# Relaying the opening of a fused attention and feed-forward kernel

## Chip, cores and metric

The kernel runs on one NeuronCore of a Trainium2 chip. The metric is the device time of one execution in microseconds (us), taken as the median of several runs. The profile is one execution recorded by the hardware profiler; its own span is a little shorter than the measured time (431.2 us against 433.38 us).

Engines and their short names: PE (TensorE, matmuls; PEld is its weight load), DVE (VectorE), ACT (ScalarE), POOL (GpSimd), SP (SyncE, which here only issues transfers).

## What is computed

Attention with normalised queries and keys over 8 batches, 12 heads, 448 positions and 64 dimensions, and then a feed-forward layer with a leaky activation on the 3584 x 768 result:

```python
def rmsnorm(x, g):
    rms = np.sqrt(np.mean(x * x, axis=-1, keepdims=True) + 1e-06)
    return x / rms * g
q_n, k_n = (rmsnorm(q, g_q), rmsnorm(k, g_k))
scores = (1.0 / np.sqrt(64)) * np.matmul(q_n, k_n.transpose(0, 1, 3, 2))
scores = scores - np.max(scores, axis=-1, keepdims=True)
attn = np.exp(scores)
attn = attn / (np.sum(attn, axis=-1, keepdims=True) + 1e-09)
x = np.matmul(attn, v)           # then heads side by side: 3584 x 768
h = x @ w_in                     # w_in: 768 x 2048
out = np.maximum(0.01 * h, h) @ w_out   # w_out: 2048 x 768
```

## The kernel before

Work is cut into 24 **units** of four heads of one batch. A unit goes through these steps:

- load q and k (SP) and v (POOL, with a conversion to 16 bits);
- squares (`prep_sq` on ACT, `prep_sqp` on POOL), their sums (`prep_ssq`, DVE), the factor 1/rms as exp(-0.5 ln) (`prep_rinv`, two ACT instructions), the multiplication (`prep_norm`, DVE);
- transposition of the normed q and k (`prep_tr`: seven matmuls into PSUM each, then a copy to SBUF on DVE or ACT; q gets the gains on the way);
- scores in seven steps t (`qk`, PE), the exponentials of each step (`ex`, ACT). The exponential needs a shift, which is taken from the maxima of step 0: `shift_max` (DVE), a matmul that spreads it (`shift_mm`, PE), two small DVE instructions, the last of which writes `eb`;
- sums of the exponentials (`zsum`) and the product with v (`pv`), both PE; 1/sum as Ln and Exp (`zinv`, ACT); the product of both (`xmul`, DVE).

Three units make a batch, and a batch's feed-forward matmuls are then fed between the attention steps of later units. That regular loop starts with unit 3. What the change touches is the hand-laid order ahead of it, in which the scheduler is switched off: each engine runs its instructions in the order of the program text.

The helpers that the text below speaks of:

```python
raws = ctx.enter_context(tc.tile_pool(name="raws", bufs=3))   # raw q, k: 3 units
# squares: 3 buffers in turn for q and k together; normed n16: 1 buffer
n16=([P, 2, NS, 2, D], FP16, 1), ...
def aux(shape, dtype, name):                                  # PSUM: 4 banks in turn
    return psum.tile(shape, dtype, tag="aux", bufs=4, name=name)
def slot():                                                   # PSUM: 2 pairs of banks for scores
    return psum.tile([P, 2, 512], FP32, tag="sT", bufs=2, name="sT")

def prep_sq(u, c=ALL, tis=BOTH):
    for ti in tis:
        nc.scalar.activation(buf(u, f"sq{ti}")[:, :, c[0]:c[1]], raw[u][ti][:, :, c[0]:c[1]], AF.Square)

def prep_sqp(u, tis=BOTH):
    for ti in tis:
        nc.gpsimd.tensor_tensor(buf(u, f"sq{ti}"), raw[u][ti], raw[u][ti], op=ALU.mult)

def prep_norm(u, c=ALL, tis=BOTH):      # two inputs in SBUF: the raw rows and the factors
    ...
        nc.vector.tensor_tensor(buf(u, "n16")[...], src[:, :, c[0]:c[1]], buf(u, "rinv")[... broadcast], op=ALU.mult)

def prep_tr(u, ti, copies):             # all chunks through one PSUM tile
    tp = aux([P, NS, P], FP16, "tp")
    for (lo, hi), copy in copies:
        for x in range(lo, hi):
            nc.tensor.transpose(tp[:, x, :], buf(u, "n16")[:, ti, x]..., ident16)
        copy(buf(u, "qkT")[:, ti, lo:hi], tp[:, lo:hi], ti == 0)

def gate(u):    # POOL copies the last element of the normed k: what follows on POOL waits for it
    nc.gpsimd.tensor_copy(gate_t, buf(u, "n16")[:, 1, NS - 1, 1, D - 1:D])

def warm(n, bank):                      # n matmuls whose result is not used
    for x in range(n):
        nc.tensor.matmul(bank[:, P:2 * P], onesp, onesp, start=True, stop=True)

def score0(u):                          # step 0 of the scores, in two aux banks
    banks = [aux([P, 512], FP32, "s0") for a in range(2)]
    score(u, 0, banks)
    st[u]["sT"] = [(0, banks)]
```

The opening itself can be read from the minus and blank-led lines of the diff below; CA, CB, K0 and K1 are chunks of the seven tiles of a unit: 0 to 3, 4 to 6, 0 alone, and 1 to 6.

Of the kernel before, what the change touches and what calls it, by code (L numbers as in the profile page):

```python
# [18 lines left out]
def kernel(  # L19
# [35 lines left out]
    def aux(shape, dtype, name):  # L55
        return psum.tile(shape, dtype, tag="aux", bufs=4, name=name)
# [30 lines left out]
    def load_w_in(n0, n):  # L87
        for a in range(2):
            for r in range(2):
                nc.gpsimd.dma_start(win16[64 * a:64 * a + 64, :, r, n0:n0 + n], win_v[a, :, :, r, n0:n0 + n])  # L90
# [19 lines left out]
    def load_v(u):  # L110
        nc.gpsimd.dma_start(vts[u % NV].rearrange("p a t d -> p a (t d)"), rows(v, u))  # L111
# [9 lines left out]
    def buf(u, name):  # L121
        if name not in st[u]:
            shape, dtype, bufs = SHAPES[name]
            st[u][name] = prep_p.tile(shape, dtype, tag=name[:2] if bufs == 3 and name != "qkT" else name, bufs=bufs, name=name)
        return st[u][name]
# [7 lines left out]
# [3 lines that stand above are left out]
# [4 lines left out]
    def prep_ssq(u, c=ALL, tis=BOTH):  # L140
        for ti in tis:
            nc.vector.tensor_reduce(buf(u, "ssq")[:, ti, :, c[0]:c[1]], buf(u, f"sq{ti}")[:, :, c[0]:c[1]],  # L142
                                    axis=AXL.X, op=ALU.add)

    def prep_rinv(u, tis=BOTH):
        x = slice(tis[0], tis[-1] + 1)
        nc.scalar.activation(buf(u, "uu")[:, x], buf(u, "ssq")[:, x], AF.Ln, bias=eps_t, scale=1.0 / D)
        nc.scalar.activation(buf(u, "rinv")[:, x], buf(u, "uu")[:, x], AF.Exp, bias=0.0, scale=-0.5)  # L148

    def prep_norm(u, c=ALL, tis=BOTH):  # L150
        n = c[1] - c[0]
        for ti in tis:
            src = raw[u][ti]
            nc.vector.tensor_tensor(  # L154
                buf(u, "n16")[:, ti, c[0]:c[1]].rearrange("p s a d -> p a s d"), src[:, :, c[0]:c[1]],
                buf(u, "rinv")[:, ti, :, c[0]:c[1], None].broadcast_to([P, 2, n, D]), op=ALU.mult)

    def prep_tr(u, ti, copies):
# [3 lines that stand above are left out]
                nc.tensor.transpose(tp[:, x, :], buf(u, "n16")[:, ti, x].rearrange("p a d -> p (a d)"), ident16)  # L162
            copy(buf(u, "qkT")[:, ti, lo:hi], tp[:, lo:hi], ti == 0)
# [21 lines left out]
    def qk(u, steps):  # L185
        st[u]["sT"] = []
        for t in steps:
            sT = slot()
            score(u, t, (sT[:, 0], sT[:, 1]))
            st[u]["sT"].append((t, sT))  # L190

    def ex(u):
        s = st[u]
        if "et" not in s:
            s["et"] = epool.tile([P, NS, 2, S], FP16, tag="et", name="et")
        for t, sT in s["sT"]:
            if isinstance(sT, list):
                for a in range(2):
                    nc.scalar.activation(s["et"][:, t, a], sT[a][:, 0:S], AF.Exp, bias=s["eb"], scale=1.0)
            else:  # L200
                nc.scalar.activation(s["et"][:, t], sT[:, :, 0:S], AF.Exp, bias=s["eb"], scale=1.0)  # L201

    def score0(u):
# [4 lines that stand above are left out]
    def shift_max(u):  # L208
        s = st[u]
        sT = s["sT"][0][1]  # L210
        if isinstance(sT, list):
            pm2 = small.tile([P, 2], FP32, tag="pm2", name="pm2")
            for a in range(2):
                nc.vector.tensor_reduce(pm2[:, a:a + 1], sT[a][:, 0:S], axis=AXL.X, op=ALU.max)
            s["spare"] = sT[0]
            nc.vector.tensor_reduce(s["spare"][:, 511:512], pm2, axis=AXL.X, op=ALU.max)
        else:
            s["spare"] = sT[:, 0]
            nc.vector.tensor_reduce(s["spare"][:, 511:512], sT[:, :, 0:S], axis=AXL.XY, op=ALU.max)  # L219
        s["dg"] = small.tile([P, P], FP16, tag="dg", name="dg")  # L220
        nc.vector.tensor_tensor(s["dg"], ident16, s["spare"][:, 511:512].broadcast_to([P, P]), op=ALU.mult)

    def shift_bank(u):
        st[u]["pb"] = aux([P, 512], FP32, "pb")
# [17 lines left out]
    def gate(u):  # L242
        nc.gpsimd.tensor_copy(gate_t, buf(u, "n16")[:, 1, NS - 1, 1, D - 1:D])
# [11 lines left out]
    def zsum_slot(u):  # L255
        s = st[u]
        s["zslot"] = slot()
        s["zt"] = [s["zslot"][:, r] for r in range(2)]
        zsum(u)
# [48 lines left out]
    def zinv(u):  # L308
        s = st[u]
        s["rz"] = zpool.tile([P, 2, S], FP32, tag="rz", name="rz")  # L310
        if "zslot" in s:
            nc.scalar.activation(s["rz"], s["zslot"][:, :, 0:S], AF.Ln)
            nc.scalar.activation(s["rz"], s["rz"], AF.Exp, bias=0.0, scale=-1.0)
        else:
            for r in range(2):
                nc.scalar.activation(s["rz"][:, r], s["zt"][r][:, 0:S], AF.Ln)
                nc.scalar.activation(s["rz"][:, r], s["rz"][:, r], AF.Exp, bias=0.0, scale=-1.0)

    def pv(u, t0=0, t1=NS):
        s = st[u]  # L320
        if t0 == 0 and "pslot" not in s:
            s["pv"] = [aux([P, 512], FP32, "pv") for r in range(2)]
        for t in range(t0, t1):
            for r in range(2):
                for a in range(2):
                    nc.tensor.matmul(s["pv"][r][64 * a:64 * a + 64, 0:S], vts[u % NV][64 * r:64 * r + 64, a, t],  # L326
                                     s["et"][64 * r:64 * r + 64, t, a], start=(t == 0), stop=(t == NS - 1))
# [244 lines left out]
    def warm(n, bank):  # L572
        for x in range(n):
            nc.tensor.matmul(bank[:, P:2 * P], onesp, onesp, start=True, stop=True)

    with tc.manual_schedule():
# [19 lines left out]
        nc.vector.tensor_copy(gcol, gps[:, 0:1])  # L596
        prep_ssq(0, ALL, (1,))
        prep_rinv(0, (1,))
        prep_sqp(1, (0,))
        load_v(0)  # L600
        load_v(1)
        prep_norm(0, CA, (0,))
        prep_norm(0, CB, (0,))
        prep_tr(0, 0, ((CA, acopy), (CB, acopy)))
        prep_norm(0, K0, (1,))
        tpk = aux([P, NS, P], FP16, "tp")

        def trk(c, copy):
            for x in range(*c):
                nc.tensor.transpose(tpk[:, x, :], buf(0, "n16")[:, 1, x].rearrange("p a d -> p (a d)"), ident16)  # L610
            copy(buf(0, "qkT")[:, 1, c[0]:c[1]], tpk[:, c[0]:c[1]])

        trk(K0, vcopy)
        prep_norm(0, K1, (1,))
        qk(0, STEPS[0])
        shift_max(0)
        trk(K1, acopy)
        load(3)
        prep_sqp(1, (1,))
        gate(0)  # L620
        load_w_in(0, 1024)
        prep_sqp(2)
        shift_bank(0)
        warm(12, st[0]["pb"])
        shift_mm(0)
        load_v(2)
        prep_ssq(1, ALL, (0,))

        def feed(u):
            load(u + 4)  # L630
            gate(u + 1)
            prep_sqp(u + 3)
            load_v(u + 3)

        def trn(u, ti, copy):
            prep_tr(u, ti, ((ALL, copy),))
# [2 lines left out]
            zsum(u, t0, t1)  # L639
            pv(u, t0, t1)  # L640

        def close(u):
            n = u + 1
            zsum_slot(u)
            ex(n)
            qk(n, (1,))
            pv(u)
            zinv(u)

        ex(0)  # L650
        prep_ssq(1, ALL, (1,))
        prep_rinv(1)
        prep_norm(1)
        prep_ssq(2)
        feed(0)
        load_w_in(1024, 1024)
        wb = aux([P, 512], FP32, "warm")
        qk(0, (1,))
        ex(0)
        warm(16, wb)  # L660
        qk(0, (2,))
        ex(0)
        warm(12, wb)
        qk(0, (3,))
        ex(0)
        warm(6, wb)
        qk(0, (4,))
        ex(0)
        trn(1, 0, vcopy)
        trn(1, 1, acopy)  # L670
        qk(0, (5,))
        ex(0)
        qk(0, (6,))
        ex(0)
        prep_rinv(2)
        score0(1)
        shift_max(1)
        shift_bank(1)
        warm(20, st[1]["pb"])
        shift_mm(1)  # L680
        close(0)

        prep_norm(2)
        prep_ssq(3)
        ex(1)
        feed(1)
        for f in range(2):
            load_w_out(8 * f, 8)
# [8 lines left out]
        ex(1)  # L697
        qk(1, (5,))
        ex(1)
        prep_rinv(3)  # L700
        score0(2)
        shift_max(2)
        qk(1, (6,))
# [1 line left out]
        shift_bank(2)  # L705
        warm(12, st[2]["pb"])
        shift_mm(2)
        close(1)

        prep_norm(3)  # L710
        ex(2)
        feed(2)
        qk(2, (2,))
        ex(2)
# [133 lines left out]
```

The softmax here doesn't subtract the row's maximum and nothing guards it: scores larger than these inputs give would overflow.

## Time and profile before

| | |
|---|---|
| measured time | 433.38 us, median of 3 runs (433.32 to 433.84) |
| span of the profiled execution | 431.2 us |
| PE, ACT, DVE, POOL busy | 409.3, 306.5, 273.2, 86.6 us |
| exponentials of 128x896 | 166, 1005 ns each on the mean |
| GpSimd squares of 128x896 | 1.67 to 1.82 us each |
| first exponential of unit 0, 1, 2, 3 | 17.23, 28.07, 36.99, 49.20 us |

"Busy" counts the time in which an engine executes; a transfer that an engine issues is not counted. A row of the timeline merges neighbouring instructions of one kind: its second column is then their busy time together, and the number after the x says how many they are. The bracket at its end gives how long the engine stood idle before the row, and whose result ended that. The column of the granted clock is the share of its full clock that TensorE was given. The share of the DMA comes out over 1 in some windows.

### The profile page before, as it was taken

The numbers are of one execution on the slowest core, as the hardware profiler recorded it, in microseconds if no ns is written. First come the engines' busy times: TensorE is split into PE (matmuls) and PEld (weight loads), VectorE is DVE, ScalarE is ACT, GpSimd is POOL, SyncE is SP. The second block draws the span as 40 slices with busy tenths as digits, with TensorE's granted clock in tenths as the row PEclk, the third lists the DMA queues.
The fourth block names the chain that finished last, engine by engine and source line by source line (L and its number), as shares of the span: only waits on it lengthen the run. The fifth ranks groups of instructions, "written<-read, shape, count | busy, mean of one in ns | idle before, by whom it ended". The sixth has DMA issues, their size and how long they took to land.

```text
span 431.2 us, 8844 instructions
## 1 busy us (share of the span) xinstructions
PE 409.3 (95%) x3645; PEld 211.2 (49%) x3645; DVE 273.2 (63%) x434; ACT 306.5 (71%) x466; POOL 86.6 (20%) x77
## 2 busy tenths in 40 slices
PE   7677999999989999999999999999999999999996
PEld 6545444445444544454445544454445444455553
DVE  5898656888659865487369864587359840542162
ACT  5389888757986779966986789966986757643400
POOL 2885423300002102112102102111101101010000
PEclk9699999999999999999999999999999999999999
DMA  8999993789566896578555797488572460212013
GB/s 264 198 239 252 237 254 85 143 170 221 154 104 114 194 206 161 143 128 212 156 103 136 170 209 171 130 141 194 160 109 44 118 143 16 44 38 73 2 44 103
DMA packets 66476, 62.37 MB, mean 145 GB/s; under 512 B 35716, under 2 KB 61572, under 8 KB 66436
## 3 DMA queue, kind: packets, MB, share of 16 engines
q1 hardware_dynamic: 55840, 49.62, 46.7%
q0 software_dynamic: 10272, 11.80, 17.8%
q8 instruction: 28, 0.46, 0.4%
q10 hardware_dynamic: 324, 0.39, 0.3%
q14 instruction: 12, 0.10, 0.1%
HBM read 45.61 MB, written 11.01 MB: 131 GB/s over the span
## 4 chain that ended last, share of the span: by engine, by line
PE 63%; ACT 16%; DVE 12%; issue 3%; ACTq 0%; DVEq 0%
PE hps L347 25%; ACT et L201 8%; PE ma L427 7%; PE md L427 6%; PE sT L182 5%; PE sT L326 4%; PE op L387 4%; PE mc L427 4%; DVE n L154 3%; PE mb L427 3%; ACT gt L341 3%; PE zc L269 3%; DVE ssq L142 1%; DVE sT L219 1%; ACT x L281 1%
## 5 line engine op out<-in xcount | busy, mean ns | idle before, releaser
L201 ACT ACTIVATE et<-sT,eb 128x896 f16<-128x896 f32 x166 | 158.6, 1005 | 15.6 <-PE sT L182 13.3
L347 PE MATMUL hps<-xt,win 128*128 128x448 f16 x756 | 151.0, 353 | 0.2 <-DVE xt L335 0.2
L347 PEld LDWEIGHTS <-win 128*128 128x128 f16 x756 | 70.6, 98 | 71.4 <-issue 9.9
L341 ACT ACTIVATE gt<-hps 128x448 f16<-128x448 f32 x126 | 65.7, 541 | 20.1 <-PE hps L347 19.4
L306 POOL TENSOR_TENSOR xt<-x,rz 128x896 f16<-128x896 f32 x16 | 33.5, 2092 | 150.8 <-DMA rz<-zs 49.8
L154 DVE TENSOR_TENSOR n<-rq,rinv 128x896 f16<-128x896 f32 (+2 forms) x25 | 27.5, 1102 | 48.4 <-ACT rinv L148 44.9
L182 PE MATMUL sT<-qkT 64*64 64x448 f16 x664 | 52.6, 366 | 4.8 <-ACT et L201 4.3
L142 DVE TENSOR_REDUCE ssq<-sq 128x14 f32<-128x896 f32 (+2 forms) x49 | 50.1, 1055 | 1.2 <-ACT sq L131 1.2
L427 PEld LDWEIGHTS <-sa 128*128 128x128 f16 x352 | 32.8, 98 | 26.3 <-issue 6.1
L281 ACT COPY x<-sT 128x896 f32<-128x896 f32 x19 | 17.2, 907 | 39.5 <-DVE sT L232 39.5
L111 POOL DMA_DIRECT2D vt<-in_v_dram x24 | 18.2, 760 | 114.4 <-PE sT L326 106.9
L427 PEld LDWEIGHTS <-gt 128*128 128x128 f16 x264 | 25.2, 98 | 20.3 <-issue 4.4
L219 DVE TENSOR_REDUCE sT<-sT 128x1 f32<-128x896 f32 x22 | 24.0, 1093 | 17.5 <-PE sT L182 17.5
L182 PEld LDWEIGHTS <-qkT 64*64 64x64 f16 x672 | 15.8, 104 | 39.0 <-issue 35.9
L387 PE MATMUL op<-wout,gt 128*128 128x384 f16 x192 | 34.1, 327 | 0.0
L427 PE MATMUL ma<-wout,gt 128*128 128x384 f16 x176 | 32.3, 326 | 0.1
L154 DVE TENSOR_TENSOR n<-rk,rinv 128x896 f16<-128x896 f32 (+2 forms) x25 | 30.1, 1206 | 0.0
L326 PE MATMUL sT<-et,vt 64*64 64x448 f16 x532 | 28.5, 349 | 0.3
L408 DVE TENSOR_TENSOR sa<-gt 128x512 f16<-128x512 f16 (+1 forms) x15 | 8.1, 543 | 29.6 <-ACT gt L341 29.6
L326 PEld LDWEIGHTS <-vt 64*64 64x64 f16 x672 | 20.4, 107 | 10.8 <-issue 1.1
L387 PEld LDWEIGHTS <-gt 128*128 128x128 f16 x192 | 17.7, 98 | 14.0 <-issue 3.2
L453 ACT COPY ost<-ma 128x384 f32<-128x384 f32 x11 | 5.3, 480 | 23.6 <-PE ma L427 23.6
(87 smaller groups left out, 444.9 us busy)
## 6 DMA issues: line engine op xcount, KB each, us to landing
rq<-in_q_dram SPq DMA_DIRECT2D x24, 448.0 KB, 5.0
rk<-in_k_dram SPq DMA_DIRECT2D x24, 448.0 KB, 5.9
out_dram<-ost SPq DMA_DIRECT2D x52, 192.0 KB, 3.8
rz<-zs SPq DMA_DIRECT2D x38, 224.0 KB, 3.3
vt<-in_v_dram POOLq DMA_DIRECT2D x24, 224.0 KB, 5.0
win<-in_moe_w_in_dram POOLq DMA_DIRECT2D x8, 384.0 KB, 9.4
wout<-in_moe_w_out_dram POOLq DMA_DIRECT2D x2, 1536.0 KB, 23.7
out_dram<-ost SPq DMA_DIRECT2D x4, 96.0 KB, 2.1
```

What stands on the lines that cost most here:

```text
L142: nc.vector.tensor_reduce(buf(u, "ssq")[:, ti, :, c[0]:c[1]], buf(u, f"sq{ti}")[:, :, c[0]:c[1]], axis=AXL.X, op=ALU.add)
L154: nc.vector.tensor_tensor(buf(u, "n16")[:, ti, c[0]:c[1]].rearrange("p s a d -> p a s d"), src[:, :, c[0]:c[1]], buf(u, "rinv")[:, ti, :, ...
L182: nc.tensor.matmul(banks[a][64 * r:64 * r + 64, 0:S].rearrange("p (t x) -> p t x", t=NS), kT(u, r, a, t), qT(u, r, a), start=True, stop=True)
L201: nc.scalar.activation(s["et"][:, t], sT[:, :, 0:S], AF.Exp, bias=s["eb"], scale=1.0)
L219: nc.vector.tensor_reduce(s["spare"][:, 511:512], sT[:, :, 0:S], axis=AXL.XY, op=ALU.max)
L281: nc.scalar.copy(s["x32"], s["pslot"][:, :, 0:S])
L306: eng.tensor_tensor(xts[b][:, g], s["x32"], s["rz"], op=ALU.mult)
L326: nc.tensor.matmul(s["pv"][r][64 * a:64 * a + 64, 0:S], vts[u % NV][64 * r:64 * r + 64, a, t], s["et"][64 * r:64 * r + 64, t, a], start=(t ...
L341: nc.scalar.activation(dst, src, AF.Prelu, bias=0.0, scale=1.0, alpha=0.01)
L347: nc.tensor.matmul(hps[:, 0:S], win16[:, kt // 2, kt % 2, ts(ft, P)], xt[:, kt // 2, kt % 2], start=(kt == 0), stop=(kt == KT - 1))
L387: nc.tensor.matmul(op2[:, 0:HC], gt[:, ft, ds(col(t), P)], wout16[:, ft, ds(HC * half, HC)], start=(ft == 0), stop=(ft == FT - 1))
L427: nc.tensor.matmul(bank[:, 0:HC], a[:, f], b[:, f], start=(first and f == 0), stop=(f == HF - 1), skip_group_check=not first)
```

## The change

It reorders the opening, from unit 0's norms to the start of unit 2's exponentials:

- **GpSimd gated.** Its first squares, those of unit 1, are taken from it; its first instruction after the set-up is now the gate on unit 0's norms. The squares of unit 1 are computed on ACT. The loads of v and of w_in are put at other places of POOL's queue: v of unit 0 ahead of the squares of unit 2, v of units 1 and 2 after the first half of w_in, the second half of w_in ahead of the squares of unit 3.
- **Transposes through separate tiles.** The two chunks of unit 0's q get a PSUM tile each, and its k is normed in full ahead of the copy of its first tile. In unit 1 the copy of q moves from DVE to ACT and k is handled in two chunks on DVE.
- **Shifts earlier.** The step 0 scores and the shift of unit 1 are computed among the exponentials of unit 0; the sums, factors and norms of unit 2 come after the shift of unit 1 instead of before, and so with unit 3 and unit 2.
- **Fewer warm-up matmuls.** 20 fewer ahead of the shift of unit 1, 6 fewer ahead of that of unit 0, and others moved.

The diff, whole:

```diff
--- before.py
+++ after.py
@@ -596,35 +596,39 @@
         nc.vector.tensor_copy(gcol, gps[:, 0:1])
         prep_ssq(0, ALL, (1,))
         prep_rinv(0, (1,))
-        prep_sqp(1, (0,))
-        load_v(0)
-        load_v(1)
         prep_norm(0, CA, (0,))
         prep_norm(0, CB, (0,))
-        prep_tr(0, 0, ((CA, acopy), (CB, acopy)))
         prep_norm(0, K0, (1,))
-        tpk = aux([P, NS, P], FP16, "tp")
-
-        def trk(c, copy):
-            for x in range(*c):
-                nc.tensor.transpose(tpk[:, x, :], buf(0, "n16")[:, 1, x].rearrange("p a d -> p (a d)"), ident16)
-            copy(buf(0, "qkT")[:, 1, c[0]:c[1]], tpk[:, c[0]:c[1]])
-
-        trk(K0, vcopy)
         prep_norm(0, K1, (1,))
+
+        def tr(u, ti, chunks, tp=None):
+            if tp is None:
+                tp = aux([P, NS, P], FP16, "tp")
+            for c, copy in chunks:
+                for x in range(*c):
+                    nc.tensor.transpose(tp[:, x, :], buf(u, "n16")[:, ti, x].rearrange("p a d -> p (a d)"), ident16)
+                copy(buf(u, "qkT")[:, ti, c[0]:c[1]], tp[:, c[0]:c[1]], ti == 0)
+            return tp
+
+        tr(0, 0, ((CA, acopy),))
+        tr(0, 0, ((CB, acopy),))
+        tpk = tr(0, 1, ((K0, vcopy),))
+        prep_sq(1, ALL, (0,))
         qk(0, STEPS[0])
         shift_max(0)
-        trk(K1, acopy)
+        tr(0, 1, ((K1, acopy),), tpk)
+        prep_sq(1, ALL, (1,))
         load(3)
-        prep_sqp(1, (1,))
         gate(0)
+        load_v(0)
+        prep_sqp(2)
         load_w_in(0, 1024)
-        prep_sqp(2)
+        load_v(1)
+        load_v(2)
         shift_bank(0)
-        warm(12, st[0]["pb"])
+        warm(6, st[0]["pb"])
         shift_mm(0)
-        load_v(2)
-        prep_ssq(1, ALL, (0,))
+        prep_ssq(1)
 
         def feed(u):
             load(u + 4)
@@ -639,50 +643,48 @@
             zsum(u, t0, t1)
             pv(u, t0, t1)
 
-        def close(u):
-            n = u + 1
-            zsum_slot(u)
-            ex(n)
-            qk(n, (1,))
-            pv(u)
-            zinv(u)
-
         ex(0)
-        prep_ssq(1, ALL, (1,))
-        prep_rinv(1)
-        prep_norm(1)
-        prep_ssq(2)
-        feed(0)
-        load_w_in(1024, 1024)
-        wb = aux([P, 512], FP32, "warm")
+        prep_rinv(1, (0,))
         qk(0, (1,))
         ex(0)
-        warm(16, wb)
+        prep_rinv(1, (1,))
+        prep_norm(1, ALL, (0,))
+        prep_norm(1, K0, (1,))
+        prep_norm(1, K1, (1,))
+        load(4)
+        gate(1)
+        load_w_in(1024, 1024)
+        prep_sqp(3)
+        load_v(3)
+        wb = aux([P, 512], FP32, "warm")
+        warm(12, wb)
         qk(0, (2,))
         ex(0)
-        warm(12, wb)
+        warm(16, wb)
         qk(0, (3,))
+        tr(1, 0, ((ALL, acopy),))
+        tpk = tr(1, 1, ((K0, vcopy),))
         ex(0)
-        warm(6, wb)
         qk(0, (4,))
         ex(0)
-        trn(1, 0, vcopy)
-        trn(1, 1, acopy)
+        tr(1, 1, ((K1, vcopy),), tpk)
+        score0(1)
+        shift_max(1)
         qk(0, (5,))
         ex(0)
         qk(0, (6,))
         ex(0)
+        shift_bank(1)
+        shift_mm(1)
+        prep_ssq(2)
+        ex(1)
+        qk(1, (1,))
+        ex(1)
+        zsum_slot(0)
+        pv(0)
         prep_rinv(2)
-        score0(1)
-        shift_max(1)
-        shift_bank(1)
-        warm(20, st[1]["pb"])
-        shift_mm(1)
-        close(0)
-
+        zinv(0)
         prep_norm(2)
-        prep_ssq(3)
-        ex(1)
         feed(1)
         for f in range(2):
             load_w_out(8 * f, 8)
@@ -697,7 +699,6 @@
         ex(1)
         qk(1, (5,))
         ex(1)
-        prep_rinv(3)
         score0(2)
         shift_max(2)
         qk(1, (6,))
@@ -705,10 +706,16 @@
         shift_bank(2)
         warm(12, st[2]["pb"])
         shift_mm(2)
-        close(1)
+        prep_ssq(3)
+        ex(2)
+        qk(2, (1,))
+        ex(2)
+        zsum_slot(1)
+        pv(1)
+        prep_rinv(3)
+        zinv(1)
 
         prep_norm(3)
-        ex(2)
         feed(2)
         qk(2, (2,))
         ex(2)
```

## Prediction

> **What bounds the kernel now.** I read the busy shares first, then the windows table, to see where the bounding engine is not full, and then the merged timeline of that part.
>
> The first page section says that TensorE is busy for 95% of the span:
>
> ```profile
> span 431.2 us, 8844 instructions
> PE 409.3 (95%) x3645; PEld 211.2 (49%) x3645; DVE 273.2 (63%) x434; ACT 306.5 (71%) x466; POOL 86.6 (20%) x77
> ```
>
> The table of windows (columns: window, length, busy time of PE, PEld, DVE, ACT, POOL with counts, granted clock, DMA share, GB/s) separates two regimes:
>
> ```profile
> 10.00:20.00 10.00, 6.15 (x54) 4.59 (x55) 7.94 (x10) 3.04 (x6) 9.07 (x11) 0.66 0.95 202
> 20.00:30.00 10.00, 7.88 (x126) 5.22 (x128) 9.12 (x14) 8.36 (x12) 7.84 (x10) 1.00 1.12 240
> 30.00:40.00 10.00, 7.88 (x136) 4.72 (x125) 8.31 (x15) 9.79 (x15) 6.81 (x8) 1.00 1.11 248
> ...
> 229.00:289.00 60.00, 59.52 (x533) 29.50 (x532) 41.52 (x68) 47.56 (x70) 9.87 (x8) 1.00 0.71 151
> ```
>
> From about 49 us PE is busy 59.5 of 60 us: PE alone bounds it. Before that PE waits, and part of its work is warm-up matmuls. There the exponentials on ACT should be the bound, but ACT is busy for only 3.0 us between 10 and 20 us. The change touches only this opening. If the opening ends X us sooner, and nothing later runs short, the kernel ends X us sooner. So I follow four milestones, the first exponentials of units 0 to 3, in the timeline (columns: start, duration, engine, line, operation, out<-in, count, idle before it and its releaser):
>
> ```profile
> 8.50 1.82 POOL L135 TENSOR_TENSOR sq<-rq 128x896 f32<-128x896 f32 x1 [7.18 <-DMA rq<-in_q_dram]
> 8.69 1.77 DVE L154 TENSOR_TENSOR n<-rk,rinv 128x128 f16<-128x128 f32 x1
> 10.92 3.48 DVE L154 TENSOR_TENSOR n<-rk,rinv 128x768 f16<-128x768 f32 x1
> 11.89 1.69 POOL L135 TENSOR_TENSOR sq<-rk 128x896 f32<-128x896 f32 x1
> 14.33 1.09 DVE L219 TENSOR_REDUCE sT<-sT 128x1 f32<-128x896 f32 x1
> ...
> 17.23 1.01 ACT L201 ACTIVATE et<-sT,eb 128x896 f16<-128x896 f32 x1 [1.12 <-DVE eb L240]
> ...
> 28.07 1.16 ACT L199 ACTIVATE et<-s,eb 128x448 f16<-128x448 f32 x2 [1.61 <-DVE eb L240]
> ...
> 36.99 1.16 ACT L199 ACTIVATE et<-s,eb 128x448 f16<-128x448 f32 x2
> ...
> 49.20 1.01 ACT L201 ACTIVATE et<-sT,eb 128x896 f16<-128x896 f32 x1 [1.09 <-DVE eb L240]
> ```
>
> The DVE norm of 128 columns took 1.77 us and that of 768 columns 3.48 us, while the 896-column norms elsewhere take 1.08 to 1.09 us. Both long ones end right after a GpSimd square does (10.32 and 13.58 us). The score maximum stands behind them until 14.33 us.
>
> [...] 3.48 us is the wait until 13.58 plus 0.8 us of own work. [...] the trace has 951 ns for the square of 896. [...] the trace shows 0.66 in the window where PE stood still from 11.4 to 14.5 us.
>
> **The change, milestone by milestone.** Durations are those of the same rows in the trace before: exponential 0.92 us each in a row (4.58/5), Ln and Exp of the sums 1.82 us, ln/exp pair of one norm factor 0.45 to 0.55 us, sum of squares 1.03 us, norm 1.09 us, square on GpSimd 1.69 us.
>
> *Unit 0, first exponential.* Without GpSimd's squares the 128- and 768-column norms take about 0.25 and 0.93 us (0.8 of work plus start). DVE: norms done at 8.7 + 0.25 + 0.93 = 9.85 us, copy of K0 until 10.05. ACT's second copy of q no longer waits for the first to free the transposing tile and ends near 9.98. Scores at 10.1 instead of 11.06, maximum at 10.55 instead of 14.33, and 2.25 us from its start to the exponential (1.09, then diagonal, matmul, reduction, bias; 1.12 as in later units): **12.8** instead of 17.23. ACT meanwhile does the new squares, 0.95 each, and the K1 copy, 0.8: 9.98 + 0.9 + 1.05 + 0.95 = 12.75 us; just hidden. Gain 4.4.
>
> *Unit 0 to 1.* ACT: 7 x 0.92 + two pairs of norm factors (1.0) + the copy of q (0.92) + about 0.8 of waiting = 9.1 us. The wait: GpSimd's second square of unit 2 needs the buffer that the first sum of unit 1 frees (13.85), so it runs 13.9 to 15.6; the norm of q of unit 1, ready at 14.85, waits for it and ends at 16.7; its transposes and copy end at 18.25, while the third exponential ended at 16.65. The shift of unit 1: copies done at 19.1, then 2.57 us (as 25.50 to 28.07 before) = 21.65, under the last exponential, which ends at 21.9. First exponential of unit 1 at **21.9** instead of 28.07. Period 9.1 against 10.84, gain 1.7. The missing 20 warm-up matmuls cost nothing, if the clock stays up.
>
> *Unit 1 to 2.* Here the change gives something back. The sums and factors of unit 2 now come after the shift of unit 1, so its norms start at 21.9 + 2.1 (three exponentials) + 0.6 (factors) = 24.65, that is 2.7 us into the unit; before, 0.15 us ahead of it. DVE then: two norms to 26.75, two copies to 28.0, xmul to 29.15, and 2.50 us from the score maxima to the exponential (34.49 to 36.99 before): **31.65**. ACT would be done at 31.0. Period 9.75 against 8.92: loss 0.8.
>
> *Unit 2 to 3.* The factors of unit 3 move into this unit (0.55 on ACT), and its norms, at 34.35 to 36.45, now end after Ln and Exp (36.1), so the scores behind their transposes hold one exponential up by 0.55: period 12.2 + 1.1 = 13.3. First exponential of unit 3 at **45.0** instead of 49.20.
>
> Sum without a further collision: 4.4 + 1.7 - 0.8 - 1.1 = 4.2 us.
>
> *A likely collision.* The second half of w_in now stands on GpSimd ahead of the squares of unit 3, and its last two issues wait until the first two quarters of the first half have landed. Issued at 15.6 us, with 6.7 to 8 us to landing as before, that is 23 to 25 us; the squares then run in 23.5 to 28, across the norms of unit 2 (24.65 to 26.75), on the DVE chain that sets the next milestone. If DVE is first, nothing; if GpSimd gets in between, 1.7 us; if both squares go first, up to 3. I take 1.2. Expected gain **3.0**: 433.4 - 3.0 is about 430.3 us.
>
> The PE instructions after the opening are the same in the same order, so I carry the gain through unchanged.
>
> **Rivals.** (1) *DMA is the bound of the opening*: its share is over 1.0 from 20 us on, so the data could come no sooner. Against it: in the waits up to 62 us DMA holds up only the first squares (7.2 us on GpSimd, which is not on the path, and 1.2 and 0.5 us on ACT). But the DMA engines idle near 15 us in the new order, as w_in is issued 1 us later. If w_in or w_out were late, the gain would be gone: about 433. w_out landed at 54 and 63.5 us and the second half is first needed near 78, so there are 14 us of room. (2) *GpSimd collides repeatedly* in units 1 and 2 and the clock falls for want of warm-up: gain 0 to 1. (3) *No collision*, and waits that I counted are hidden: 427.5 to 429. (4) *PE rate after the opening absorbs it*: only if units 3 and 4 wait for sums or loads; they now have fewer us of lead on DVE.
>
> **Range and chances.** 4.2 without the collision and 1.2 with it at its worst bracket the centre; with 0.8 us for my reading of the chains on each side, 428.2 to 432.6 us. 2% would be 8.7 us, more than the whole of what the opening waits for (ACT's waits between 8 and 50 us add up to 11 us, of which 4.8 and 1.6 are attacked), so faster by over 2% gets 0.03. Slower by 2% would take two new long waits: 0.01. Within 2%: 0.96.
>
> **What would show it.** The norms of unit 0 at 0.25 and 0.93 us; first exponentials near 12.8, 21.9, 31.7 to 33, and 45 to 46.5 us; a norm of unit 1 of about 1.8 us beside a GpSimd square; the norms of unit 2 at 24.6 us, long if GpSimd's squares of unit 3 fall there; PE busy 59.5 of 60 us afterwards and the same distance from unit 3's first exponential to the end (382 us). Wrong it would be if that distance grows, which would mean late weights or late norms, or if the clock is at half in units 0 and 1.

## The result and the profile after

The changed kernel takes 431.9 us (median of 4 runs, 431.43 to 432.87) against 433.35 us before; the ratio is 0.9972, with a 95% interval of 0.9956 to 0.9989. It is faster by 1.45 us on the medians (0.5 to 1.9 us by the interval), about half of what was predicted, though the time itself lies inside the predicted range.

The head of the profile page of the changed kernel shows a shorter span and PE as busy as before:

```profile
span 430.1 us, 8784 instructions
PE 410.4 (95%) x3613; PEld 209.2 (49%) x3613; DVE 271.8 (63%) x436; ACT 308.7 (72%) x470; POOL 83.1 (19%) x75
```

The merged timeline of its opening (start, duration, engine, line, operation, out<-in, count, idle before it and releaser) has the rows that answer to those shown of before (rows between them are left out):

```profile
8.84 1.15 DVE L154 TENSOR_TENSOR n<-rk,rinv 128x128 f16<-128x128 f32 x2
10.62 1.10 DVE L219 TENSOR_REDUCE sT<-sT 128x1 f32<-128x896 f32 x1 [0.49 <-PE sT L182]
12.99 1.01 ACT L201 ACTIVATE et<-sT,eb 128x896 f16<-128x896 f32 x1 [0.30 <-DVE eb L240]
14.03 1.68 POOL L135 TENSOR_TENSOR sq<-rk 128x896 f32<-128x896 f32 x1 [1.26 <-DVE ssq L142]
14.86 1.79 DVE L154 TENSOR_TENSOR n<-rq,rinv 128x896 f16<-128x896 f32 x1
...
22.56 1.19 ACT L199 ACTIVATE et<-s,eb 128x448 f16<-128x448 f32 x2
...
23.67 0.63 POOL L90 DMA_DIRECT2D win<-in_moe_w_in_dram  x1 [2.05 <-DMA win<-in_moe_w_in_dram]
24.31 1.69 POOL L135 TENSOR_TENSOR sq<-rq 128x896 f32<-128x896 f32 x1
25.20 3.40 DVE L154 TENSOR_TENSOR n<-rq,rinv 128x896 f16<-128x896 f32 x1 [1.15 <-issue]
25.95 1.69 POOL L135 TENSOR_TENSOR sq<-rk 128x896 f32<-128x896 f32 x1
28.52 1.08 DVE L154 TENSOR_TENSOR n<-rk,rinv 128x896 f16<-128x896 f32 x1
...
34.36 1.16 ACT L199 ACTIVATE et<-s,eb 128x448 f16<-128x448 f32 x2 [0.97 <-DVE eb L240]
...
48.14 1.01 ACT L201 ACTIVATE et<-sT,eb 128x896 f16<-128x896 f32 x1 [1.09 <-DVE eb L240]
```

The two norms of unit 0's k now take 1.15 us together, where they had taken 1.77 and 3.48. The first exponentials of units 0 and 1 come 4.2 and 5.5 us sooner than before. Then the gain melts: 2.6 us at unit 2, 1.1 us at unit 3. The row that stands out is the norm of q of unit 2, at 25.20 us: 3.40 us for what takes 1.09 us elsewhere. It ends at 28.60, that is 0.96 us after GpSimd's second square (25.95 + 1.69 = 27.64). From unit 3's first exponential to the end it is 430.1 - 48.14 = 382.0 us, as before (431.2 - 49.20 = 382.0); in the profiles of all runs below it is 381.9 to 382.4 us. Whatever the opening gains or loses is passed on whole.

A second thing stands out. The windows of one us of the changed kernel (the third column from the end is the granted clock, the second number after the window PE's busy time) show half the clock twice, at 11.3 to 18.1 us and at 21.5 to 28.3 us:

```profile
12.00:13.00 1.00, 0.84 (x7) 0.26 (x7) 0.61 (x4) 0.70 (x2) 0.77 (x1) 0.50 0.91 266
...
19.00:20.00 1.00, 0.38 (x4) 0.12 (x5) 0.98 (x2) 1.00 (x3) 1.00 (x3) 1.00 1.01 158
...
24.00:25.00 1.00, 1.00 (x19) 0.57 (x14) 0.04 (x1) 0.97 (x3) 0.98 (x2) 0.50 1.12 244
```

The kernel before was at half clock once in its opening, from 13.2 to 20.0 us, so only the second stretch is new:

```profile
15.00:16.00 1.00, 1.00 (x12) 1.00 (x11) 0.70 (x2) 0.68 (x1) 1.00 (x3) 0.50 0.62 74
```

In the second stretch the sums and the product with v of unit 0 take 2.83 and 2.87 us, against 1.49 us each for those of unit 1 at full clock (33.94 and 35.26 us). So there were two theories of the lost gain. **Collision**: GpSimd's squares of unit 3 keep DVE off the norms of unit 2. **Clock**: with fewer warm-up matmuls (32 fewer in all, 3613 PE instructions against 3645) the clock falls and PE is late.

### The profile page after: what moved, and what is told of

It reads as the page before. It is cut to its first block, busy times and chain, and to the rows that moved or that the text cites. A ratio compares the mean times of both kernels' runs of the same rounds, so it can differ in the third digit from the quotient of the medians.

```text
span 430.1 us, 8784 instructions
## 1 busy us (share of the span) xinstructions
PE 410.4 (95%) x3613; PEld 209.2 (49%) x3613; DVE 271.8 (63%) x436; ACT 308.7 (72%) x470; POOL 83.1 (19%) x75
## 4 chain that ended last, share of the span: by engine, by line
PE 65%; ACT 15%; DVE 13%; issue 4%; DMA 2%; SPq 0%; DVEq 0%; ACTq 0%
PE hps L347 25%; ACT et L201 8%; PE ma L427 7%; PE sT L182 6%; PE md L427 6%; DVE n L154 5%; PE sT L326 4%; PE op L387 4%; PE mc L427 4%; PE mb L427 3%; ACT gt L341 3%; PE zc L269 2%; DVE sT L219 1%; DVE ssq L142 1%; DMA rk<-in_k_dram 1%
## 5 line engine op out<-in xcount | busy, mean ns | idle before, releaser
L154 DVE TENSOR_TENSOR n<-rq,rinv 128x896 f16<-128x896 f32 (+2 forms) x25 | 29.9, 1201 | 50.8 <-ACT rinv L148 46.2
L427 PEld LDWEIGHTS <-sa 128*128 128x128 f16 x352 | 32.8, 98 | 26.3 <-issue 6.1
L182 PEld LDWEIGHTS <-qkT 64*64 64x64 f16 x672 | 15.6, 105 | 39.4 <-issue 35.5
L326 PEld LDWEIGHTS <-vt 64*64 64x64 f16 x672 | 21.4, 109 | 11.9 <-issue 1.7
L154 DVE TENSOR_TENSOR n<-rk,rinv 128x896 f16<-128x896 f32 (+2 forms) x26 | 26.1, 1009 | 0.0
L453 ACT COPY ost<-ma 128x384 f32<-128x384 f32 x11 | 5.3, 478 | 23.6 <-PE ma L427 23.6
```

The costliest lines, as they stand in the source:

```text
L154: nc.vector.tensor_tensor(buf(u, "n16")[:, ti, c[0]:c[1]].rearrange("p s a d -> p a s d"), src[:, :, c[0]:c[1]], buf(u, "rinv")[:, ti, :, ...
L182: nc.tensor.matmul(banks[a][64 * r:64 * r + 64, 0:S].rearrange("p (t x) -> p t x", t=NS), kT(u, r, a, t), qT(u, r, a), start=True, stop=True)
L427: nc.tensor.matmul(bank[:, 0:HC], a[:, f], b[:, f], start=(first and f == 0), stop=(f == HF - 1), skip_group_check=not first)
```

## The experiments

All times below are medians. A ratio is that of the mean times, to the kernel before run on the same chip, with its 95% interval in brackets; one execution of 2279 us, of the run with the squares of unit 1 back on GpSimd, is left out of its ratio.

### Which of the two: warm-up, or the squares elsewhere, or both

Warm-up matmuls put back around the last two score steps of unit 0:

```diff
         shift_max(1)
+        shift_bank(1)
+        warm(9, st[1]["pb"])
         qk(0, (5,))
         ex(0)
+        warm(8, st[1]["pb"])
         qk(0, (6,))
         ex(0)
-        shift_bank(1)
+        warm(3, st[1]["pb"])
         shift_mm(1)
```

> The changed kernel with 20 warm-up matmuls again around the last two score steps of unit 0. Clock theory (the half clock from 21.2 to 28.2 us costs the time): the clock stays full there, the sums and the product with v of unit 0 take 1.5 us each instead of 2.83 and 2.87, the first exponential of unit 1 comes near 22.0 instead of 22.56 and that of unit 2 near 33, and the time falls by about 1.3 us to 430.6. Collision theory (GpSimd's two squares of unit 3 hold the norms of unit 2 up, and they set the next milestone): the norms still end near 29.5 and the first exponential of unit 2 stays at 34.0 to 34.4, time 431.5 to 431.9.

Measured: 432.8 us, ratio 0.9991 (0.9979 to 1.0003). The clock did stay up from 18.4 to 28.7 us, and the first exponential of unit 1 came at 22.30. The norm of q of unit 2 still took 3.83 us, and the first exponential of unit 2 came at 35.27 us, not sooner:

```profile
24.93 3.83 DVE L154 TENSOR_TENSOR n<-rq,rinv 128x896 f16<-128x896 f32 x1 [1.01 <-issue]
...
35.27 1.16 ACT L199 ACTIVATE et<-s,eb 128x448 f16<-128x448 f32 x2 [0.77 <-DVE eb L240]
```

PE was not busy at all from 26 to 28 us, while the norm of q stood, and the clock was at half from 28.7 to 32.1 us instead. Holding the clock from 18.4 to 28.7 us gained nothing; the time is above what either theory had forecast.

The squares of unit 3 ahead of the second half of w_in:

```diff
         gate(1)
-        load_w_in(1024, 1024)
         prep_sqp(3)
+        load_w_in(1024, 1024)
         load_v(3)
```

> The changed kernel with the squares of unit 3 ahead of the second half of w_in in GpSimd's queue. Collision theory: the squares run at 19.8 to 21.5 and 23.1 to 24.8, the norms of unit 2 take 1.09 us each from 25.2 on, and the first exponential of unit 2 comes 2.3 us sooner, near 32.0; time 429.6. Clock theory: PE, at half clock until 28.2, reaches the transposes of unit 2 only then, so that at most 1 us is gained: first exponential of unit 2 at 33.3 to 34.3, time 430.9 to 431.8.

Measured: 428.89 us, ratio 0.9901 (0.9877 to 0.9925). Its timeline:

```profile
22.52 1.68 POOL L135 TENSOR_TENSOR sq<-rk 128x896 f32<-128x896 f32 x1 [0.99 <-DVE ssq L142]
24.47 1.09 DVE L154 TENSOR_TENSOR n<-rq,rinv 128x896 f16<-128x896 f32 x1 [1.03 <-POOL sq L135]
...
31.67 1.16 ACT L199 ACTIVATE et<-s,eb 128x448 f16<-128x448 f32 x2 [0.53 <-DVE eb L240]
```

The square is over at 24.20, the norm takes 1.09 us, and the milestone of unit 2 falls at 31.67 instead of 34.36 us, that of unit 3 at 45.45 instead of 48.14. This swap of two lines is worth twice the whole change. The clock was at half here too, from 10.8 to 14.2 and 21.0 to 24.4 us.

Both edits:

> Both edits. If each hides the other: first exponential of unit 1 near 22.0, of unit 2 near 31.7, of unit 3 near 45.3, time 429.0 (the blind sum was 4.2 us without a collision). If neither is the cause: as the changed kernel, 431.9.

Measured: 429.11 us, ratio 0.9903 (0.9886 to 0.9921), first exponentials of units 1 to 3 at 22.12, 31.61 and 45.39 us. With the collision gone, the warm-up adds nothing that can be measured.

### Is it the collision, or the order of the loads?

Moving the squares ahead also moved the issue of w_in's second half, which began at 24.14 instead of 19.76 us. So the squares were moved the other way, behind the gate on unit 2's norms, with w_in in its place:

```diff
         load_w_in(1024, 1024)
-        prep_sqp(3)
         load_v(3)
 ...
         prep_norm(2)
-        feed(1)
+        load(5)
+        gate(2)
+        prep_sqp(3)
+        prep_sqp(4)
+        load_v(4)
```

> The changed kernel with the squares of unit 3 moved the other way: behind the gate on unit 2's norms. The second half of w_in keeps its place, so this separates the collision from the order of the loads. Collision theory: the norms of unit 2 take 1.09 us each, the first exponential of unit 2 comes at 31.6 to 32.3 and the time is 428.6 to 429.5, as with the squares moved ahead. Load-order rival (the earlier run gained because w_in came later and left the DMA to q and k): the norms may be short, but the time stays at 431.5 or more.

Measured: 428.98 us, ratio 0.9897 (0.9877 to 0.9917); norms 1.09 and 1.08 us, unit 2 at 31.42, unit 3 at 45.14 us:

```profile
24.25 1.09 DVE L154 TENSOR_TENSOR n<-rq,rinv 128x896 f16<-128x896 f32 x1 [1.05 <-issue]
25.26 1.08 DVE L154 TENSOR_TENSOR n<-rk,rinv 128x896 f16<-128x896 f32 x1
...
31.42 1.16 ACT L199 ACTIVATE et<-s,eb 128x448 f16<-128x448 f32 x2 [0.52 <-DVE eb L240]
```

The last part of w_in's second half was issued at 23.62 us, as in the changed kernel (23.67). The order of the loads is not the cause.

With only the square of k behind the gate, and that of q left where it was:

```diff
         load_w_in(1024, 1024)
-        prep_sqp(3)
+        prep_sqp(3, (0,))
 ...
         gate(2)
+        prep_sqp(3, (1,))
         prep_sqp(4)
```

> The changed kernel with only the square of k of unit 3 behind the gate; that of q stays at 24.3 us. If DVE waits for as many squares as stand ahead of it, the norm of q of unit 2 waits about 0.75 us (it ends near 27.1 instead of 28.6) and the first exponential of unit 2 comes near 32.5: time 429.8, between the other two. [...]

Measured: 430.22 us, ratio 0.9924 (0.9904 to 0.9944). Its timeline:

```profile
24.14 1.69 POOL L135 TENSOR_TENSOR sq<-rq 128x896 f32<-128x896 f32 x1
24.24 2.56 DVE L154 TENSOR_TENSOR n<-rq,rinv 128x896 f16<-128x896 f32 x1 [1.04 <-issue]
...
32.55 1.16 ACT L199 ACTIVATE et<-s,eb 128x448 f16<-128x448 f32 x2 [0.97 <-DVE eb L240]
```

The norm ends at 26.80, 0.97 us after the one square (25.83), and unit 2 begins 1.1 us later than without any square in the way. None, one and two squares give 31.42, 32.55 and 34.36 us. In this run the clock was full from 8 to 36 us, so a falling clock has no part in its 1.1 us.

### The clock with the collision in place

The changed kernel with GpSimd's order as it was and more warm-up: 8 more at the start, 12 ahead of unit 0's scores, the 20 of the first run, and 24 ahead of unit 2's transposes.

```diff
-        warm(42, wbank)
+        warm(50, wbank)
 ...
+        warm(12, wbank)
         qk(0, STEPS[0])
 ...
         qk(1, (2,))
         ex(1)
+        warm(24, st[1]["pb"])
         trn(2, 0, vcopy)
```

> The changed kernel, GpSimd's order as it was, with enough warm-up matmuls to hold TensorE's clock at full through units 0 and 1 (8 more at the start, 12 ahead of unit 0's scores, 20 around its last score steps, 24 ahead of unit 2's transposes). It isolates the clock with the collision in place. Collision theory: both squares of unit 3 still hold the norm of q of unit 2 for 2.3 us, first exponential of unit 1 near 21.7 and of unit 2 near 33.8, time 431.0 to 431.5. If the clock was half of the loss: unit 2 at 32.5 or earlier, 430 or less.

Measured: 432.77 us, ratio 0.9991 (0.9976 to 1.0006), above the 431.0 to 431.5 expected. The clock was full up to 28.3 us and then at half until 31.7, so the run does not hold it through the whole of unit 1. Its timeline:

```profile
21.24 1.18 ACT L199 ACTIVATE et<-s,eb 128x448 f16<-128x448 f32 x2
...
23.73 1.69 POOL L135 TENSOR_TENSOR sq<-rq 128x896 f32<-128x896 f32 x1
23.87 4.14 DVE L154 TENSOR_TENSOR n<-rq,rinv 128x896 f16<-128x896 f32 x1 [1.02 <-issue]
25.37 1.69 POOL L135 TENSOR_TENSOR sq<-rk 128x896 f32<-128x896 f32 x1
...
34.33 1.16 ACT L199 ACTIVATE et<-s,eb 128x448 f16<-128x448 f32 x2 [0.76 <-DVE eb L240]
```

Unit 1 begins 1.3 us sooner than in the changed kernel, the norm is issued 1.3 us sooner, but it waits longer and ends only 0.6 us sooner (28.01 instead of 28.60). The norm again ends 0.95 us after the second square (27.06), and the squares began when GpSimd's queue had waited 1.99 us for w_in to land: more than half of the time won ahead of it is lost there. Unit 2 begins at 34.33, as in the changed kernel (34.36); I had expected 33.8. The other 0.6 us went between the norm and the exponential: 6.32 us here and 6.51 in the first run, where the clock fell to half behind the standing norm, against 5.75 to 5.76 in the three runs with a held norm and a full clock there (the changed kernel, the one with one square behind the gate, the one with the squares of unit 1 back). So more warm-up ahead of the norm did not help: in both runs PE was not busy from 26 to 28 us, behind the norm, and the clock fell at about the norm's end (norm 28.01 and 28.76, clock 28.3 and 28.7 us).

### One part alone, and one part undone

The kernel before with unit 1's squares on ScalarE and the loads of v of units 0 and 1 behind the gate, and nothing else:

```diff
-        prep_sqp(1, (0,))
-        load_v(0)
-        load_v(1)
 ...
         trk(K0, vcopy)
+        prep_sq(1, ALL, (0,))
 ...
-        prep_sqp(1, (1,))
+        prep_sq(1, ALL, (1,))
         gate(0)
+        load_v(0)
+        load_v(1)
```

> The kernel before with one part of the change alone: squares of unit 1 on ScalarE, v of units 0 and 1 loaded after the gate. If taking GpSimd off the norms of unit 0 carries the gain, the first exponential of unit 0 comes near 13.3 instead of 17.23, and with the old order from there on all later milestones move by 3 to 3.5 us: 24.7, 33.6, 45.8; time 430.0, below the changed kernel. If the later order of the change is needed to keep it, the next milestones take it back: first exponential of unit 1 at 26.5 or later, time 432 or more.

Measured: 432.65 us, ratio 0.9984 (0.9976 to 0.9993). First exponentials at 13.31, 26.68, 35.92 and 48.59 us: 3.9 us are won in unit 0 and most is given back in unit 1. Its timeline shows how:

```profile
15.34 1.69 POOL L135 TENSOR_TENSOR sq<-rq 128x896 f32<-128x896 f32 x1
15.96 2.03 DVE L154 TENSOR_TENSOR n<-rq,rinv 128x896 f16<-128x896 f32 x1 [0.70 <-issue]
16.98 2.54 POOL L135 TENSOR_TENSOR sq<-rk 128x896 f32<-128x896 f32 x1
17.92 2.56 DVE L154 TENSOR_TENSOR n<-rk,rinv 128x896 f16<-128x896 f32 x1
```

The squares of unit 2 had been clear of most of unit 1's norms, which took 1.55 and 1.08 us in the kernel before; with the norms 4 us sooner both of them collide (2.03 and 2.56 us). The clock also was at half from 19.4 to 26.3 us here, so that not all of the 2.5 us given back in unit 1 is shown to be the collision's.

The changed kernel with the squares of unit 1 back on GpSimd, behind the gate:

```diff
-        prep_sq(1, ALL, (0,))
 ...
-        prep_sq(1, ALL, (1,))
         load(3)
         gate(0)
+        prep_sqp(1)
         load_v(0)
```

> The changed kernel with the squares of unit 1 back on GpSimd, behind the gate. If moving them to ScalarE carries part of the gain: they run from 10.2 to 13.6, those of unit 2 end near 17, the norms of unit 1 wait for them, and the first exponential of unit 1 comes at 23.5 to 24.5 instead of 22.56; unit 2 near 36, time 432.5 to 434. If the gate alone carries it: 431.9 as the changed kernel.

Measured: 434.42 us, ratio 1.0022 (1.0012 to 1.0033), slower than before and a little above the range expected. The first exponential of unit 0 is as early as ever (12.37 us), but GpSimd is behind: the norm of q of unit 1 takes 3.84 us, that of unit 2 4.16 us, and unit 1 begins at 23.25, unit 2 at 35.82 us. Moving the squares to ScalarE was needed as well as the gate.

The kernel before without its 20 warm-up matmuls ahead of unit 1's shift:

```diff
         shift_bank(1)
-        warm(20, st[1]["pb"])
         shift_mm(1)
```

> The kernel before without the 20 warm-up matmuls ahead of unit 1's shift. If they hold the clock: it falls to half near 25 to 28 us, the sums and the product with v take 2.8 us each, and the first exponential of unit 2 comes 0.5 to 1.5 us later than 36.99; time up to 434.5. If the clock stays up without them, as the prediction assumed for the changed kernel: 433.2, no change.

Measured: 433.43 us, ratio 1.0005 (0.9993 to 1.0016): no difference that can be measured. The clock in its profile fell to half at 29 to 32 us and was full again after, and unit 2 came 9.85 us after unit 1 instead of 8.92. The profiled execution was also slow to start (first exponential at 18.58 instead of 17.23 us), because its k came later: ACT's square of k stands at 6.90 instead of 5.64 us, and DVE's first norm at 8.89 instead of 7.62. (GpSimd's two squares then caught the norms of q, 1.86 us for 512 columns and 3.21 for 384, instead of those of k.) The profile alone would have misled; by the interval of the times these matmuls are worth 0.7 us at most.

### A better version

Squares of unit 3 ahead of w_in, and the square of k of unit 2 written, in 16 bits, into a tile that is not yet used, so that it need not wait for a buffer:

```diff
+        st[2]["sq1"] = gt[:, 0:2, 0:NS * D].rearrange("p a (t d) -> p a t d", d=D)
         prep_sqp(2)
```

> The version with the squares of unit 3 ahead of w_in, and the square of k of unit 2 written (in 16 bits) into the still unused gt tile, so that it need not wait for the sum of unit 1. The remaining collision in unit 0 (norm of q of unit 1: 1.80 us) goes: norm of q 1.09 us, ending near 16.0, and later milestones 0.7 us sooner, time 428.2. If TensorE's clock or the exponentials bound unit 0 by then, less than 0.2 us: 428.7 to 429.

Measured: 428.62 us, ratio 0.9890 (0.9863 to 0.9918). The norm of q of unit 1 took 1.51 us, as the square, waiting for its data, ran until 14.90. With the warm-up of the clock run added, but for the 24 ahead of unit 2's transposes (+8, +12 and +20 matmuls):

> The same with 8 more warm-up matmuls at the start, 12 ahead of unit 0's first scores and 20 around the last score steps of unit 0, to hold the clock. If the clock costs anything by itself: full clock from 8 to 34 us, first exponential of unit 1 near 21.0 and 0.3 to 0.6 us better than without, time 427.7. If not: as the version without, within 0.3 us.

Measured: 428.28 us, ratio 0.9879 (0.9861 to 0.9897). The clock was full from 8 to 36 us, the norm of unit 1 took 1.08 us. Then the scores of step 3 of unit 2 were put ahead of unit 3's transposes:

```diff
         qk(2, (2,))
         ex(2)
+        qk(2, (3,))
+        ex(2)
         trn(3, 0, vcopy)
         trn(3, 1, vcopy)
         xmul(1)
         prep_ssq(4)
-        qk(2, (3,))
-        ex(2)
```

> The best version so far (squares of unit 3 ahead of w_in, spare buffer, warm-up) with the scores of step 3 of unit 2 ahead of unit 3's transposes. ScalarE waited 0.49 us twice in unit 2 behind those transposes; if that wait is on the path, the first exponential of unit 3 comes 0.4 to 0.9 us sooner than 44.6 and the time is 427.5; if DVE (two norms, copies, products and sums in a row) sets it, 428.3 as before.

Measured: 428.4 us, ratio 0.9883 (0.9864 to 0.9903). ACT's two waits of 0.5 us each behind those transposes became one of 1.08 us, a step later. The intervals of these three versions and of the swap alone overlap: the swap is what is shown to pay, and the rest, 0.5 to 1.0 us by the ratios, is not shown. All four beat both kernels.

## Why the prediction was wrong

- **What bounds the kernel; a gain in the opening is a gain at the end.** Right: 382.0 us follow unit 3's first exponential in both profiles, so the PE work behind it did not absorb the gain (rival 4).
- **Unit 0.** Right: the norms took 1.15 us together (predicted 0.25 and 0.93), the first exponential came at 12.99 (12.8).
- **Unit 0 to 1.** Nearly right: the collision with unit 2's square was there as worked out (1.79 us, end near 16.7), but the first exponential of unit 1 came at 22.56, not 21.9. The step "cost nothing, if the clock stays up" had its condition unmet: the clock fell twice. The prediction had set the granted clock of 0.66 beside a standstill of PE from 11.4 to 14.5 us, but here PE was busy for 0.42, 0.42, 0.41 and 0.82 of each us from 7 to 11 us, with no gap over 1.09 us, and the clock fell at 11.3 all the same. What makes it fall is not shown. Where the clock was full until 20.7 us or longer, in the three runs with the same GpSimd order in unit 0, it came at 21.2 to 21.6. The lateness did not matter, since the next milestone did not depend on it.
- **The uncollided sum, 4.2 us.** Right: with the squares moved either way, units 2 and 3 begin at 31.4 to 31.7 and 45.1 to 45.5 us (predicted 31.65 and 45.0), and the time is 428.9 to 429.0 (433.4 - 4.2 = 429.2). One term was short: unit 2 to 3 takes 13.7 to 13.8 us in these runs, not 13.3. ACT waits twice for the scores behind the transposes, 0.4 to 0.5 us each, where one wait of 0.55 was counted.
- **The likely collision: this is the step that failed.** The place, the two instructions and the cause (GpSimd's queue waiting for w_in, though only its last issue waited, for 2.05 us) were as written; the size was not. I listed three outcomes (0, 1.7 and up to 3 us), estimates from the 1.69 us of one square, weighed them and took 1.2. My own figures, squares from 23.5 us and norms from 24.65, already had GpSimd first and left little for the outcome 0. Measured, the squares started at 24.31 and the norm at 25.20, and the second square followed the first without a gap. The worst outcome came in each of the four profiles with this order (the changed kernel, the two with warm-up, the one with squares back): norms of 3.40, 3.83, 4.14 and 4.16 us. That the norm would stand through both squares could not be told beforehand: in the run with the gate alone it ended at 17.99 us, ahead of the second square (19.52). The sums, counted at their usual 1.03 us, were not held up: two took 2.07 us beside squares in the kernel before (from 17.11 us), and 2.07 us with none beside them in the changed kernel (from 21.97 us). On the milestones the collision cost 2.7 to 2.9 us in unit 2. So 4.2 - 1.2 = 3.0 should have been about 4.2 - 2.8 = 1.4, and 1.45 us was measured.
- **Rivals.** DMA as a bound: no, two orders of the same loads gave 428.9 and 429.0 us. Repeated collisions with a falling clock (gain 0 to 1): the collisions were real, and the clock fell, but it was not the loss: the swap gave 428.9 us with the clock at half in two stretches. A half clock in units 0 and 1 had been named as a sign of being wrong; the sign came, but it was not the reason. No collision (427.5 to 429): that is what the swap made of it.
- **Slips in the sums.** 8.7 + 0.25 + 0.93 is 9.88, not 9.85. 9.98 + 0.9 + 1.05 + 0.95 is 12.88, not 12.75, which would no longer be hidden behind 12.8; measured, the last of these squares ended at 12.69, 0.30 us ahead of the exponential. 6.7 to 8 us after 15.6 is 22.3 to 23.6, not 23 to 25. 433.4 - 3.0 is 430.4, not 430.3. The landing alone bears on the outcome: put right, it speaks still more for GpSimd being first.

## What to carry to other kernels

Where instructions of two engines hold each other up, as norms and squares did here (a norm of 1.09 us took 2.56 us with one square in the way and 3.40 to 4.16 with two), and both are ready at nearly the same time, work out which is ready first and with how many instructions in a row, and reckon with the whole row, rather than average the outcomes; and if that hangs on the landing of a transfer, take the landing as part of the chain. GpSimd's squares stood in its queue behind an issue that waited 2.05 us for a transfer, and putting them ahead of it brought the time from 431.9 to 428.9 us: put the arithmetic that others depend on, or collide with, ahead of such issues. After every gain in an early stage, list again what the other engines do at the new times; moving the norms of unit 1 four us forward put them under squares that had been nearly harmless (1.55 and 1.08 us before, 2.03 and 2.56 with the gate alone).

## What was not expected of the hardware

Whether a norm on DVE got in between two squares on GpSimd was not settled by which had waited longer. In the changed kernel and three others a norm that had waited since the first square stood through the second as well (3.40 to 4.16 us), while in the run with the gate alone the engines alternated (norm 2.03 us, then the square 2.54, then the norm 2.56). What decides this stayed open.

The same PE instructions were granted different clocks. The changed kernel and the version with the squares behind the gate have the same PE instructions in the opening, but the first was at half clock from 11.3 to 18.1 us and the second at full clock until 20.7 us; their first exponentials of unit 1 differ by 0.9 us (22.56 and 21.62) for that reason as far as the profiles show. The run with only one square behind the gate has these PE instructions too, and stayed at full clock from 8 to 36 us (unit 1 at 21.60).
